# Bucketed attention and a feed-forward block: scores kept negated, a least in place of maximum and guard

## The chip, the cores and the metric

One of the eight cores of a Trainium2 chip runs the whole program. The metric is the device time of one execution in microseconds; a kernel's figure is the median of its timed runs. TensorE multiplies matrices from SBUF into PSUM, VectorE and ScalarE work on either memory, GpSimd only on SBUF, and SyncE issues most of the transfers. Each engine has its own queue of instructions and works it off in order; the engines wait for one another through semaphores.

## The reference

```python
batch, n_heads, seq, head_dim = (4, 8, 768, 64)         # q, k, v: float32; proj: 64 x 6
q_bits = (np.einsum('bhsd,dk->bhsk', q, proj) > 0).astype(np.int64)
k_bits = (np.einsum('bhsd,dk->bhsk', k, proj) > 0).astype(np.int64)
q_bucket = np.sum(q_bits * powers, axis=-1)             # six sign bits make a bucket
k_bucket = np.sum(k_bits * powers, axis=-1)
mask = q_bucket[:, :, :, None] == k_bucket[:, :, None, :]
scores = scale * np.matmul(q, k.transpose(0, 1, 3, 2))  # scale = 1/8
scores = np.where(mask, scores, -1000000000.0)
scores = scores - np.max(scores, axis=-1, keepdims=True)
attn = np.exp(scores)
attn = attn / (np.sum(attn, axis=-1, keepdims=True) + 1e-09)
attn_out = np.matmul(attn, v)
x = attn_out.transpose(0, 2, 1, 3).reshape(3072, 512)
h = x @ w_in                                            # 512 x 2048
g = 0.5 * h * (1.0 + erf(h / sqrt(2)))
out = g @ w_out                                         # 2048 x 512
```

A row of queries whose bucket holds no key has every score at -1e9; after the subtraction all are 0, and the row attends to all keys alike.

## The kernel before

**Tiles and stages.** The four batches follow one another, each with eight heads. For each head the function `head_early` (first batch) or `head` (the others) loads the transposed queries and keys, splits them into a rounded part and a remainder (tiles Aq, Ak, Bq, Bk), projects them on the hash vectors, takes the signs, and writes 12 further rows behind the 64 of Aq and Ak. These rows add 0 to a score where the buckets agree and a multiple of `-BIG` (2^34) where they do not. The constants are `fold`, which scales the query half by 1/8, and `off`, `flips` and the hash tiles.

A *unit* is one head's block of 128 queries, 192 in all. `unit` (line 872) lays down these steps: `scores`, four matmuls into a PSUM buffer `s` of two banks, of which there are two (line 887); `top`, the negated row maximum over 768 keys on VectorE (line 890), written to a spare column of the same buffer; `guard`, a second VectorE operation (line 894), which compares that maximum with `limit` (BIG/2) and leaves two columns in `rows`: factor 1 and the negated maximum, or 0 and 0 for a row without a key; `exps`, the exponential on ScalarE with this factor and bias as operands in memory and an accumulated row sum (line 900). The buffer `s` is free again after the exponential. In the first batch (`WHOLE`) the exponentials stay float32 and are transposed by TensorE (line 951); half a row block at a time, they are copied out of PSUM by ScalarE or VectorE (`affine`, lines 429 and 432). In the other batches they are divided by their sum, split into two float16 parts (lines 429, 432, 915) and transposed by DMA (line 922). `values` multiplies them with v (lines 1031, 1040).

The feed-forward block works on 256 tokens and half of the 2048 hidden units at a time: 24 groups of 96 matmuls with `w_in` (line 1243), Gelu on ScalarE, a split into float16 parts (lines 429, 432 and 1300), 48 matmuls with `w_out` (line 1322). The weights are decoded, scaled and split on VectorE during the first batches (lines 524 to 593).

**What sets the order.** The order is computed before the program is built. Every step is added to a `Plan` with an engine (or a choice of engines with a cost on each), a cost in microseconds, a key, the steps it needs and the buffer it takes. `Plan.order` then runs a list scheduler: whenever an engine is free it takes, of the steps that are ready, the one with the lowest key. The keys are made from the unit's number and the entries of the dictionary `PAR` (line 34): `QK`, `MX` and `EX` stand for scores, maximum, and guard with exponential. The order that comes out is each engine's instruction stream; at run time semaphores hold it to the data. So a changed cost or key can move steps on any engine, and can move a step with a choice, such as a copy, from one engine to another.

Of the kernel before, what the change touches and what calls it, by code (L numbers as in the profile page):

```python
# [10 lines left out]
F32 = mybir.dt.float32  # L11
# [217 lines left out]
def tile_bucket_attention_moe(  # L229
# [10 lines left out]
    nc = tc.nc  # L240
# [26 lines left out]
    NT = 8  # L267
# [32 lines left out]
    rows = const.tile([P, NT, 5], F32, tag="rows", name="rows")  # L300
# [30 lines left out]
    def buf(step):  # L331
        if bufs[step.takes][step.slot] is None:
            bufs["x"][step.slot] = ring(const, "x", [P, 2, NPAIR, TC], F16, 1, step.slot)[0]
        return bufs[step.takes][step.slot]
# [16 lines left out]
    limit = const.tile([P, 2], F32, tag="limit", name="limit")  # L351
    nc.gpsimd.memset(limit, BIG / 2)
    SPARE = 1000
    for t in bufs["s"]:
        nc.vector.memset(t[:, SPARE : SPARE + 1], 1.0)

    fold = const.tile([P, 1], F32, tag="fold", name="fold")
    nc.gpsimd.memset(fold[:D], SCALE)
    nc.gpsimd.memset(fold[D:], 1.0)

# [18 lines left out]
    for n, rr in enumerate((slice(0, D), slice(D, P))):  # L379
        twice = praw[rr, :NBIT].unsqueeze(1).to_broadcast([D, 2, NBIT])  # L380
        low, high = (
            hashes[rr, r0 + n * KR : r0 + n * KR + 2 * NBIT].rearrange("p (t b) -> p t b", t=2) for r0 in (0, D)
        )
        nc.gpsimd.tensor_copy(out=high, in_=twice)
        nc.gpsimd.tensor_tensor(out=low, in0=twice, in1=high.bitcast(F32), op=ALU.subtract)
# [7 lines left out]
        out=flips[KR:, 1:2], in0=flips[KR:, 0:1], scalar1=-BIG / 2, scalar2=-BIG / 2, op0=ALU.mult, op1=ALU.add  # L393
    )
    nc.gpsimd.tensor_scalar(
        out=flips[KR:, 0:1], in0=flips[KR:, 0:1], scalar1=BIG, scalar2=0.0, op0=ALU.mult, op1=ALU.add
# [302 lines left out]
    def head_early(b, h, i, key, clear, cl):  # L699
# [52 lines left out]
        lq = add_low(bq[D:], top, SCALE)  # L752
# [5 lines left out]
        for c0, c1 in ((0, TC), (TC, S)):  # L758
# [9 lines left out]
            def sign(n=n, box=box):  # L768
                nc.scalar.activation(
                    out=buf(space)[:HR, n], in_=buf(box[0])[:HR, : n.stop - n.start], func=AF.Sign, bias=off[:HR],  # L770
                )
# [8 lines left out]
        def mask_k():  # L780
            rows = buf(space)[KR : KR + 2 * NBIT]
            affine(r2.engine, ak[D : D + 2 * NBIT], rows, BIG / 2, -BIG / 2)
# [89 lines left out]
    def unit(t, i, qs, cl, whole, made, place):  # L872
# [3 lines left out]
        sc, nb, ssum, si, r = (st[:, k : k + 1] for k in range(5))  # L876

        def both(step):

            return buf(step).rearrange("p (b k) -> p b k", b=2)[:, :, : S // 2]  # L880
# [8 lines left out]
        def top():  # L889
            nc.vector.tensor_reduce(out=buf(sp)[:, SPARE + 1 : SPARE + 2], in_=both(sp), axis=AX.XY, op=ALU.max, negate=True)  # L890

        def guard():

            nc.vector.scalar_tensor_tensor(  # L894
                out=st[:, :2], in0=limit, scalar=buf(sp)[:, SPARE + 1 : SPARE + 2],
                in1=buf(sp)[:, SPARE : SPARE + 2], op0=ALU.is_gt, op1=ALU.mult,
            )

        def exps():
            nc.scalar.activation(  # L900
                out=buf(ex).rearrange("p (b k) -> p b k", b=2), in_=both(sp), func=AF.Exp, scale=sc, bias=nb,
                accum_out=sums[:, t : t + 1] if whole else ssum,
            )
# [24 lines left out]
        mx = add("DVE", 0.87, top, t - PAR[f"MX{cl}"], [sp])  # L928
        sh = add("DVE", 0.13, guard, t - PAR[f"EX{cl}"], [mx])
        ex = add("ACT", 0.98, exps, t - PAR[f"EX{cl}"], [sh], takes="p", table="exp")  # L930
# [483 lines left out]
```

## Time and profile before

| | |
|---|---|
| timed runs (3) | 875.90, 877.86, 878.99 us; median 877.86 |
| profiled execution | 875.6 us from first to last instruction (span) |
| TensorE matmuls | busy 837.4 us, 96% |
| VectorE | busy 692.7 us, 79%, 1345 instructions |
| ScalarE | busy 623.9 us, 71%, 1033 instructions |
| GpSimd | busy 186.9 us, 21% |
| transfers | 117.96 MB, 135 GB/s on average |

The profile's own time is its span; what lies before the first and after the last instruction is in the timed runs and not in it. PE is TensorE, DVE VectorE, ACT ScalarE, POOL GpSimd, SP SyncE; L890 is line 890. "Busy" is the time in which at least one instruction of the engine runs. Instructions of one engine overlap at their ends, so what one costs its engine is read from its start to the next one's start, which is less than its length.

### The profile page before, as it was taken

To read this page: it belongs to the slowest core of one execution; us is meant where nothing else is said; L and a number is where in the kernel's file an instruction comes from. 1 tells how busy PE (TensorE), PEld (TensorE's weight loads), DVE (VectorE), ACT (ScalarE), POOL (GpSimd) and SP (SyncE) were. 2 spreads that over 40 slices of the span, in tenths; PEclk is the share of its full clock that TensorE was granted. 3 is DMA by queue.
4 is the path that set the end of the run, shared out by engine and by line. 5 is a ranking of instruction groups with operands and counts; after the bars stand their busy time and mean duration, and the time that the engine had idled before them with its cause. 6 is when DMAs were issued, how large, how long until landed. Compare 5 with 4: busy or idle time off the path is not lost.

```text
span 875.6 us, 16917 instructions
## 1 busy us (share of the span) xinstructions
PE 837.4 (96%) x6428; PEld 610.5 (70%) x6428; DVE 692.7 (79%) x1345; ACT 623.9 (71%) x1033; POOL 186.9 (21%) x214
## 2 busy tenths in 40 slices
PE   3887998999999999999999999999999999999997
PEld 2766666776777776876777867777687687666663
DVE  8999999999998999898998998788888874112122
ACT  5878788788788888798878887768868764322321
POOL 6144332245323223031121112202112000000000
PEclk9999999999999999999999999999999999999999
DMA  8564654464889997777988896767677593000000
GB/s 270 190 168 145 191 147 127 109 144 77 178 176 165 211 210 146 156 137 133 190 169 173 168 184 128 141 150 146 112 162 133 110 168 73 25 1 25 1 25 24
DMA packets 270641, 117.96 MB, mean 135 GB/s; under 512 B 228768, under 2 KB 253344, under 8 KB 270560
## 3 DMA queue, kind: packets, MB, share of 16 engines
q1 hardware_dynamic: 270384, 116.88, 61.4%
q8 instruction: 50, 0.82, 0.4%
q14 instruction: 31, 0.25, 0.1%
q10 hardware_dynamic: 176, 0.00, 0.0%
HBM read 41.95 MB, written 6.29 MB: 55 GB/s over the span
## 4 chain that ended last, share of the span: by engine, by line
PE 76%; DVE 15%; ACT 3%; DMA 2%; issue 2%; POOL 1%; SPq 0%; ACTq 0%; DVEq 0%; POOLq 0%
PE hp L1322 27%; PE hp L1243 27%; PE s L887 12%; PE hp L1040 7%; DVE s L890 4%; ACT p L900 1%; PE hp L839 1%; PE hp L840 1%; DVE Win L593 1%; DVE Wout L529 1%; DVE rows L894 1%; DMA wbits<-w_in 1%; DMA pt<-hl 1%; DVE g L1300 1%; PE hp L1031 1%
## 5 line engine op out<-in xcount | busy, mean ns | idle before, releaser
L1243 PE MATMUL hp<-x,Win 128*128 128x256 f16 x2304 | 268.2, 273 | 0.0
L1322 PE MATMUL hp<-Wout,g 128*128 128x512 f16 x1152 | 265.8, 380 | 0.5 <-DVE g L1300 0.5
L1243 PEld LDWEIGHTS <-Win 128*128 128x128 f16 x2304 | 219.4, 98 | 42.0 <-issue 12.9
L1322 PEld LDWEIGHTS <-g 128*128 128x128 f16 x1152 | 106.1, 98 | 127.0 <-issue 13.4
L890 DVE TENSOR_REDUCE s<-s 128x1 f32<-128x768 f32 x192 | 180.9, 957 | 10.2 <-PE s L887 8.4
L900 ACT ACTIVATE p<-s,rows 128x768 f32<-128x768 f32 x147 | 145.1, 987 | 27.7 <-DVE rows L894 21.6
L887 PE MATMUL s<-Ak,Aq 128*128 128x384 f32 x360 | 138.8, 385 | 12.0 <-ACT p L900 10.6
L1300 DVE SCALAR_TENSOR_TENSOR g<-h,ffs,g 128x512 f16<-128x512 f32 x96 | 74.0, 781 | 83.5 <-ACT g L429 79.9
L887 PE MATMUL s<-Bk,Bq 128*128 128x384 f32 x360 | 122.2, 339 | 0.0
L1253 ACT ACTIVATE h<-hp,ffs 128x512 f32<-128x512 f32 x96 | 65.5, 683 | 79.2 <-PE hp L1243 78.8
L887 PEld LDWEIGHTS s<-Ak,Aq 128*128 128x128 f32 x360 | 68.4, 190 | 29.2 <-ACT p L900 19.0
L1040 PE MATMUL hp<-pt,vhl 128*64 128x256 f16 x1296 | 76.5, 274 | 1.8 <-DVE vhl L688 1.8
L1040 PEld LDWEIGHTS <-vhl 128*64 128x64 f16 x1296 | 68.5, 110 | 11.3 <-issue 8.9
L887 PEld LDWEIGHTS s<-Bk,Bq 128*128 128x128 f32 x360 | 68.7, 191 | 1.0
L915 DVE SCALAR_TENSOR_TENSOR wbits<-p,rows,wbits 128x768 f16<-128x768 f32 x54 | 55.4, 1027 | 1.5 <-ACT wbits L429 1.3
L915 DVE SCALAR_TENSOR_TENSOR hl<-p,rows,hl 128x768 f16<-128x768 f32 x45 | 45.7, 1018 | 5.7 <-ACT hl L429 4.8
L900 ACT ACTIVATE wbits<-s,rows 128x768 f32<-128x768 f32 x45 | 44.4, 986 | 7.2 <-PE hp L1243 3.8
L1278 ACT ACTIVATE h<-h 128x2048 f32<-128x2048 f32 (+1 forms) x25 | 46.1, 1843 | 0.4
L951 PE MATMUL hp<-ident,p 128*128 128x128 f32 x288 | 41.5, 276 | 2.7 <-DVE rb L432 1.4
L432 POOL TENSOR_SCALAR g<-h,ffs 128x512 f16<-128x512 f32 x28 | 25.0, 894 | 79.9 <-DVE rows L894 31.3
L429 ACT ACTIVATE pt<-hp 128x384 f32<-128x384 f32 x80 | 35.9, 486 | 6.5 <-PE hp L951 6.0
L432 POOL TENSOR_SCALAR Ak<-sign,flips 12x768 fp32r<-12x768 f32 x16 | 20.2, 1264 | 92.9 <-DVE sign L846 84.1
(199 smaller groups left out, 1113.5 us busy)
## 6 DMA issues: line engine op xcount, KB each, us to landing
raw<-qk SPq DMA_DIRECT2D x28, 384.0 KB, 3.8
vraw<-v SPq DMA_DIRECT2D x28, 384.0 KB, 4.2
wbits<-w_in SPq DMA_DIRECT2D x16, 512.0 KB, 4.2
wbits<-w_out SPq DMA_DIRECT2D x16, 512.0 KB, 3.6
out<-o SPq DMA_DIRECT2D x11, 512.0 KB, 2.9
Bk<-Bq SPq DMA_DIRECT2D x18, 192.0 KB, 2.7
Bq<-Aq SPq DMA_DIRECT2D x15, 192.0 KB, 3.4
Ak<-Aq SPq DMA_DIRECT2D x13, 192.0 KB, 2.9
```

Of the source, the lines that this page charges most:

```text
L432: on.tensor_scalar(out=out, in0=in_, scalar1=scale, scalar2=bias, op0=ALU.mult, op1=ALU.add)
L887: nc.tensor.matmul(to, x, y, start=k == 0, stop=k == 1)
L890: nc.vector.tensor_reduce(out=buf(sp)[:, SPARE + 1 : SPARE + 2], in_=both(sp), axis=AX.XY, op=ALU.max, negate=True)
L900: nc.scalar.activation(out=buf(ex).rearrange("p (b k) -> p b k", b=2), in_=both(sp), func=AF.Exp, scale=sc, bias=nb, accum_out=sums[:, t : ...
L915: nc.vector.scalar_tensor_tensor(out=buf(hi)[:, 1], in0=buf(ex), scalar=r, in1=buf(hi)[:, 0], op0=ALU.mult, op1=ALU.subtract,)
L951: nc.tensor.transpose(buf(step[0])[:, (k - k0) * P : (k - k0 + 1) * P], buf(ex)[:, words(k)], ident32,)
L1040: nc.tensor.matmul(pv[j * D : (j + 1) * D], buf(vh)[:, tv, kt, j * D : (j + 1) * D], buf(holds[j][0])[:, tp * KT + kt, :nt], start=kt == 0 ...
L1243: nc.tensor.matmul(buf(pair[0])[:, j * ch[1] : (j + 1) * ch[1]], win_hl[:, f0 // WB1, tw, pr, f0 % WB1 : f0 % WB1 + P], x[:, tx, pr, : ch[1]],
L1253: nc.scalar.activation(out=bufs["h"][0][:, 2 * fp : 2 * fp + 2, :nt], in_=buf(pair[0])[:, : 2 * nt].rearrange("p (j k) -> p j k", j=2), fu ...
L1278: nc.scalar.activation(out=h, in_=h, func=AF.Gelu)
L1300: nc.vector.scalar_tensor_tensor(out=gt[:, 1, s2, :nt], in0=h[:, s2, :nt], scalar=sg, in1=gt[:, 0, s2, :nt], op0=ALU.mult, op1=ALU.subtract,)
L1322: nc.tensor.matmul(buf(banks[u]), gt[:, tg, f, u * P : (u + 1) * P], wout_hl[:, ft // UT, tw, ft % UT], start=fresh and f == ti == 0, stop ...
```

## The change

The query half is scaled by -1/8 instead of 1/8, and the bucket rows change sign with it, so that PSUM holds the negated scores: small numbers where the buckets agree, and at least BIG more where they do not. One VectorE operation takes the smaller of each score and BIG/2, writes it back in place, and accumulates the least of the row into `nb`. The exponential then takes -1 as a constant factor and `nb` as its bias. A row without a key has BIG/2 everywhere, so every exponent is 0, as before. `top`, `guard`, `limit` and the spare column go. The signs of the early heads take a factor from memory (`turned`). The planner's costs for the two steps, and nearly all of its keys, are new.

```diff
-PAR = dict(DR_ACT=-182.94, DR_DVE=59.53, SI0=-589.8, SI1=-431.4, ...
+PAR = dict(DR_ACT=-116.64, DR_DVE=-333.22, SI0=-589.8, SI1=33.87, ...
...
-    rows = const.tile([P, NT, 5], F32, tag="rows", name="rows")
+    rows = const.tile([P, NT, 4], F32, tag="rows", name="rows")
...
-    limit = const.tile([P, 2], F32, tag="limit", name="limit")
-    nc.gpsimd.memset(limit, BIG / 2)
-    SPARE = 1000
-    for t in bufs["s"]:
-        nc.vector.memset(t[:, SPARE : SPARE + 1], 1.0)
...
-    nc.gpsimd.memset(fold[:D], SCALE)
+    nc.gpsimd.memset(fold[:D], -SCALE)
     nc.gpsimd.memset(fold[D:], 1.0)
+    turned = const.tile([2 * KR, 1], F32, tag="turned", name="turned")
+    nc.gpsimd.memset(turned[:KR], -1.0)
+    nc.gpsimd.memset(turned[KR:], 1.0)
...
-    for n, rr in enumerate((slice(0, D), slice(D, P))):
-        twice = praw[rr, :NBIT].unsqueeze(1).to_broadcast([D, 2, NBIT])
+    for n, (rr, n0) in enumerate(((slice(0, D), NBIT), (slice(D, P), 0))):
+        twice = praw[rr, n0 : n0 + NBIT].unsqueeze(1).to_broadcast([D, 2, NBIT])
...
-        out=flips[KR:, 1:2], in0=flips[KR:, 0:1], scalar1=-BIG / 2, scalar2=-BIG / 2, op0=ALU.mult, op1=ALU.add
+        out=flips[KR:, 1:2], in0=flips[KR:, 0:1], scalar1=BIG / 2, scalar2=BIG / 2, op0=ALU.mult, op1=ALU.add
...
-        out=flips[KR:, 0:1], in0=flips[KR:, 0:1], scalar1=BIG, scalar2=0.0, op0=ALU.mult, op1=ALU.add
+        out=flips[KR:, 0:1], in0=flips[KR:, 0:1], scalar1=-BIG, scalar2=0.0, op0=ALU.mult, op1=ALU.add
...
-        lq = add_low(bq[D:], top, SCALE)
+        lq = add_low(bq[D:], top, -SCALE)
...
-                    out=buf(space)[:HR, n], in_=buf(box[0])[:HR, : n.stop - n.start], func=AF.Sign, bias=off[:HR],
+                    out=buf(space)[:HR, n], in_=buf(box[0])[:HR, : n.stop - n.start], func=AF.Sign, scale=turned[:HR],
+                    bias=off[:HR],
...
-            affine(r2.engine, ak[D : D + 2 * NBIT], rows, BIG / 2, -BIG / 2)
+            affine(r2.engine, ak[D : D + 2 * NBIT], rows, -BIG / 2, BIG / 2)
...
-        sc, nb, ssum, si, r = (st[:, k : k + 1] for k in range(5))
+        nb, ssum, si, r = (st[:, k : k + 1] for k in range(4))
...
-        def top():
-            nc.vector.tensor_reduce(out=buf(sp)[:, SPARE + 1 : SPARE + 2], in_=both(sp), axis=AX.XY, op=ALU.max, negate=True)
-
-        def guard():
-
-            nc.vector.scalar_tensor_tensor(
-                out=st[:, :2], in0=limit, scalar=buf(sp)[:, SPARE + 1 : SPARE + 2],
-                in1=buf(sp)[:, SPARE : SPARE + 2], op0=ALU.is_gt, op1=ALU.mult,
+        def least():
+            nc.vector.tensor_scalar(
+                out=both(sp), in0=both(sp), scalar1=BIG / 2, scalar2=None, op0=ALU.min, op1=ALU.min, accum_out=nb,
             )
...
-                out=buf(ex).rearrange("p (b k) -> p b k", b=2), in_=both(sp), func=AF.Exp, scale=sc, bias=nb,
+                out=buf(ex).rearrange("p (b k) -> p b k", b=2), in_=both(sp), func=AF.Exp, scale=-1.0, bias=nb,
...
-        mx = add("DVE", 0.87, top, t - PAR[f"MX{cl}"], [sp])
-        sh = add("DVE", 0.13, guard, t - PAR[f"EX{cl}"], [mx])
-        ex = add("ACT", 0.98, exps, t - PAR[f"EX{cl}"], [sh], takes="p", table="exp")
+        mx = add("DVE", 0.96, least, t - PAR[f"MX{cl}"], [sp])
+        ex = add("ACT", 0.89, exps, t - PAR[f"EX{cl}"], [mx], takes="p", table="exp")
```

## Rows read from the trace of the kernel before

**Rows 1.** Busy us of each engine (instructions started) in stretches from:to us.
```profile
19.00:150.00 131.00, 115.29 (x852) 88.75 (x852) 128.46 (x265) 107.07 (x223) 45.27 (x44) 1.00 0.56 166
150.00:250.00 100.00, 96.24 (x748) 70.15 (x743) 95.17 (x197) 80.03 (x132) 36.72 (x37) 1.00 0.57 128
250.00:727.00 477.00, 476.23 (x3816) 353.46 (x3814) 422.85 (x810) 382.95 (x614) 93.13 (x110) 1.00 0.80 156
...
sum 876.00, PE 837.35 PEld 610.52 DVE 692.66 ACT 623.93 POOL 186.93; mean PE 139.56 PEld 101.75 DVE 115.44 ACT 103.99 POOL 31.16
```

**Rows 2.** The chain that ended last: shares of the span by engine.
```profile
PE 76%; DVE 15%; ACT 3%; DMA 2%; issue 2%; POOL 1%; SPq 0%; ACTq 0%; DVEq 0%; POOLq 0%
```

**Rows 3.** TensorE's waits from 0 to 250 us: us, times, longest.
```profile
PE s L887 <- ACT p L900: 12.2, 21, 1.3
```

**Rows 4.** Groups by line: shapes xcount | busy us, mean ns | idle before, releasers.
```profile
L890 DVE TENSOR_REDUCE s<-s 128x1 f32<-128x768 f32 x192 | 180.9, 957 | 10.2 <-PE s L887 8.4 <-PE hp L951 0.5 <-ACT diag L429 0.2
L900 ACT ACTIVATE p<-s,rows 128x768 f32<-128x768 f32 x147 | 145.1, 987 | 27.7 <-DVE rows L894 21.6 <-DVE hl L915 2.9 <-DVE tiny L409 0.8
...
L429 ACT ACTIVATE pt<-hp 128x384 f32<-128x384 f32 x80 | 35.9, 486 | 6.5 <-PE hp L951 6.0
```

**Rows 5.** The chain, 75 to 150 us: start us, us, what.
```profile
100.26 0.88 DVE s L890
...
101.17 0.23 DVE rows L894
...
113.36 0.13 DVE rows L894
```

**Rows 6.** VectorE in order of time: start us, length us, instruction.
```profile
27.07 0.97 DVE L890 TENSOR_REDUCE s<-s 128x1 f32<-128x768 f32 x1
...
28.54 0.22 DVE L894 SCALAR_TENSOR_TENSOR rows<-limit,s 128x2 f32<-128x2 f32 x1
...
39.00 0.17 DVE L991 RECIPROCAL shares<-sums 128x4 f32<-128x4 f32 x1
39.09 0.53 DVE L432 TENSOR_SCALAR pt<-hp 128x384 f32<-128x384 f32 x1
39.53 0.95 DVE L890 TENSOR_REDUCE s<-s 128x1 f32<-128x768 f32 x1
```

**Rows 7.** Groups by line and shape, as in rows 4.
```profile
L429 ACT ACTIVATE Aq<-raw,fold 128x768 fp32r<-128x768 f32 x20 | 18.6, 929 | 6.3 <-PE s L887 6.2
...
L429 ACT ACTIVATE Aq<-sign,flips 12x768 fp32r<-12x768 f32 x10 | 10.2, 1024 | 6.6 <-DVE sign L846 4.2 <-issue 1.4 <-DVE rows L909 1.0
...
L432 DVE TENSOR_SCALAR pt<-hp 128x384 f32<-128x384 f32 x16 | 8.6, 547 | 0.0
...
L432 DVE TENSOR_SCALAR rb<-hp 128x256 f32<-128x256 f32 x5 | 2.1, 412 | 0.0
```

**Rows 8.** ScalarE in order of time.
```profile
22.97 0.99 ACT L900 ACTIVATE p<-s,rows 128x768 f32<-128x768 f32 x1
23.86 0.19 ACT L900 ACTIVATION_READ_ACCUMULATOR p<-s,rows 128x1 f32 x1
23.95 0.48 ACT L429 ACTIVATE pt<-hp 128x384 f32<-128x384 f32 x1
```

**Rows 9.** The row maximum (L890) by stretch: VectorE busy us (count).
```profile
19.00:150.00 131.00, 43.28 (x46) 1.00 0.56 166
150.00:250.00 100.00, 22.55 (x24) 1.00 0.57 128
```

**Rows 10.** All engines in order of time, the first 30 us.
```profile
0.82 0.09 DVE L355 MEMSET s<- 128x1 f32 x2 [0.82 <-PEq L1403]
...
10.79 0.47 ACT L769 ACTIVATE sign<-hp,off 44x256 f32<-44x256 f32 x1 [1.36 <-PE hp L766]
```

**Rows 11.** The chain, 360 to 372 us.
```profile
361.95 1.32 PE hp L1243 x12
...
367.32 1.42 PE hp L1243 x12
```

More of the change, by code (lines that the diff above doesn't have):

```diff
@@ new lines @@
+PAR = dict(DR_ACT=-116.64, DR_DVE=-333.22, SI0=-589.8, SI1=33.87, SI2=600, SI_ACT=86.64, SI_DVE=-463.22, SI_Pool=-280.46, Z=257.45, VS0=-6.52, H0=575.6, HL=-75.74, VS=-5.3, G2=536.23, HQ=287.35, VQ=133.02, in0=-136.05, out0=39.44, in1=470.48, out1=-78.2, in2=233.28, out2=598.02, in3=240.84, out3=-463.72, H1=289.33, H2=438.91, H3=-445.9, H4=538.02, H5=-507.07, H6=-322.13, H7=-426.4, MEV=57.33, MGE=-266.31, MSP=582.63, V0=133.02, QK0=308.47, QK1=-234.44, QK2=-269.23, MX0=-109.89, MX1=-259.28, MX2=-600, EX0=477.71, EX1=387.36, EX2=-566.67, NR0=-144.91, NR1=-116.36, NR2=394.56, HI0=-417.18, HI1=144.81, HI2=-439.36, LO0=-350.93, LO1=214.11, LO2=418.95, PV0=-597.04, PV1=-520.42, PV2=-322.13, TR0=501.03, TR1=90.19, TR2=-590.8, V1=-436.5, V2=169.07, Sin0=379.14, Sin1=351.82, Sin2=508.84, Sin3=-255.14, Sout0=-176.43, Sout1=102.14, Sout2=-346.16, Sout3=188.34, Lin=269.75, Pin=377.13, Qin=-421.89, Cin=-600, Min=455.05, Lout=307.37, Pout=-115.77, Qout=-274.79, Cout=-216.53, Mout=339.83, G0=145.57, G1=316.52, G3=502.99, G4=274.38, G5=-52.33, G6=280.57, G7=-451.2, DUP0=-94.58, DUP1=-328.89, DUP2=-320.31, LOW0=-497.03, LOW1=-119.09, LOW2=500.78, PRJ0=-143.17, PRJ1=-512.55, PRJ2=-290.23, MSK0=522.69, MSK1=-11.73, MSK2=77.86, DI_ACT=-486.69, DI_DVE=100.43, DI_Pool=-394.49, WS_ACT=261.56, WS_DVE=-67.96, WS_Pool=-0.85, WH_ACT=18.86, WH_DVE=-320.98, WH_Pool=-560.31, WL_ACT=564.2, WL_DVE=-600, WL_Pool=-208.15, VH_ACT=-113.72, VH_DVE=394.66, VH_Pool=-584.38, MV_SP=-121.74, MV_ACT=138.2, MV_DVE=265.92, MV_Pool=440.5, LO_ACT=144.07, LO_DVE=311.43, LO_Pool=445.51, RND_ACT=469.84, RND_DVE=-296.69, RND_Pool=-340.91, MSK_ACT=595.62, MSK_DVE=66.63, MSK_Pool=-23.57, HI_ACT=-179.38, HI_DVE=455.51, HI_Pool=-12.15, EV_ACT=-66.36, EV_DVE=194.44, EV_Pool=-334.15, GH_ACT=120.65, GH_DVE=-153.54, GH_Pool=321.73, RB=-469.96, RS_ACT=93.05, RS_DVE=-364.96, RS_Pool=112.23, XH_ACT=-27.74, XH_DVE=-275.65, XH_Pool=11.3, XL_DVE=-458.38, XL_Pool=226.74, DUP3=-517.96, DUP4=236.89, DUP5=584.2, EX3=324.96, EX4=-372.4, EX5=-600, HI3=130.65, HI4=104.05, HI5=-279.61, LO3=430.46, LO4=479.15, LO5=45.97, LOW3=32.17, LOW4=-172.58, LOW5=-356.95, MSK3=-5.99, MSK4=311.24, MSK5=292.63, MX3=480.63, MX4=257.45, MX5=-581.8, NR3=-216.85, NR4=-574.93, NR5=345.12, PRJ3=377.13, PRJ4=180.25, PRJ5=210.32, PV3=-67.18, PV4=-452.92, PV5=211.67, QK3=89.17, QK4=399.99, QK5=99.55, SI3=266.44, SI4=573, SI5=515.21, TR3=-166.81, TR4=600, TR5=83.9, V3=111.74, V4=-181.97, V5=-188.93, Linb=328.05, Loutb=350.05, Pinb=109.11, Poutb=599.85, Qinb=259.04, Qoutb=355.37, Cinb=-101.97, Coutb=-451.52, Minb=100.86, Moutb=125.82, MVf_SP=6.12, MVf_ACT=343.18, MVf_DVE=-470.49, MVf_Pool=-600, LOf_ACT=319.76, LOf_DVE=600, LOf_Pool=-510.45, RNDf_ACT=-5.99, RNDf_DVE=-52.64, RNDf_Pool=-96.29, MSKf_ACT=-465.23, MSKf_DVE=304.16, MSKf_Pool=378.56)
```

1 line of the change is left out of this document (removed).

## The prediction

> **What bounds the kernel now.** I read busy time by stretch first [rows 1]. TensorE is busy 837.4 of the 875.6 us of the span, so all that a change off TensorE can win is 38.2 us. 15.7 of these lie between 19 and 150 us, 3.8 between 150 and 250 and 0.8 in the 477 us after that; the other 18 lie before 19 us, while the first heads are loaded and split, and at the very end. From 250 us on TensorE practically never lacks work, and a faster VectorE or ScalarE buys nothing there. From 19 to 150 us it is VectorE that is full, 128.5 of 131 us, with ScalarE at 107.1. The chain agrees: 15% of it, some 130 us, is VectorE [rows 2]. TensorE's own waits up to 250 us name the exponential that frees a scores buffer, 12.2 us in 21 waits [rows 3]; but the exponential waits for the guard, 21.6 us [rows 4], and the guard stands in VectorE's queue. So in the first stage a unit of attention is worth what it costs VectorE from the start of an operation to the start of the next.
>
> That price is read from the chain's pieces, which touch each other [rows 5]: the row maximum takes 0.88 us and, with another operation in between, its guard 0.13; 1.00 us together. Directly behind the maximum the guard starts 0.03 late and costs 0.23, since it must wait for the result. Mostly another operation stands in between, which costs the unit latency: the maximum of 27.07 us ends at 28.04, and its guard starts at 28.54 [rows 6].
>
> **The change, part by part.**
>
> *The one pass, `least`.* It goes over the same 768 elements of PSUM with one input and a constant, and writes them back. The nearest rows are VectorE's one-input copies out of PSUM: 547 ns for 384 elements and 412 for 256 [rows 7], 1.05 ns per element, so 768 last 547 + 384 x 1.05 = 950 ns, as long as the maximum's 957 [rows 4]. From start to start the 384-element copy takes 0.44 us [rows 6], so 768 take 0.44 + 0.40 = 0.84, and the maximum takes 0.88; I take 0.86. The accumulated least must also come out. The trace has no VectorE accumulator; ScalarE's exponential has one, with a row of its own, 0.19 us long, after which the next operation starts 0.09 later [rows 8]. A one-column operation of VectorE also takes 0.09 from start to start [rows 6]. So 0.86 + 0.09 = 0.95 us against 1.00: 0.05 saved per unit. The bounds: 0.14 saved if the least comes out for nothing; at the other end a write into the bank that is being read could cost a second pass, 0.80 more, so 0.75 lost. No row shows VectorE writing more than one column of PSUM. I keep 0.05, nearest to the rows of both parts. A page of the Trainium skill, "VectorE: DVE Perf Modes", in its section "Two Vector instructions with no wait between them", counts an operation that writes out its accumulator as two instructions, the pass and a read. By that rule VectorE keeps two instructions per unit, and the saving is the 0.05 already taken; without it the saving would be 0.14, and 6.4 us would stand for the first stage. No run here shows it for VectorE yet.
>
> 46 units have their maximum between 19 and 150 us, 24 up to 250 [rows 9], some 122 of the 192 after. First stage: 46 x 0.05 = 2.3 us. Where the guard stands directly behind its maximum (4 of the 46, counted along VectorE's rows; one is in [rows 5]) the wait of 0.13 goes too: 0.5 us. From 150 to 250 us VectorE is 95% busy and TensorE waits only 3.8 us; of 24 x 0.05 = 1.2 I count half, 0.6. The later units save 6 us of VectorE beside a full TensorE: nothing.
>
> *What comes earlier.* With one instruction the exponential no longer waits for a guard that is queued behind other work (0.5 us in the example of [rows 6], and 0.2 for the guard). That is latency: the scores buffer goes sooner, but VectorE has only 131 - 128.5 = 2.5 us of idle time in which to use it. Ends: 0 and 2.5; I take the middle, 1.2.
>
> *The exponential with a constant factor.* ScalarE's rows put a price on an operand held in memory: over 768 elements 929 ns with one, 1024 with two [rows 7]. The exponential has two (factor and bias) and lasts 987 [rows 4]; with one it lasts some 0.09 less, 17 us of ScalarE over 192 units. The early heads give some back: their 16 signs get a factor from memory, 16 x 0.09 = 1.4 us. In the first stage that leaves 46 x 0.09 - 1.4 = 2.7 us, on an engine with 24 us idle there. It is worth something only where the order moves VectorE's work to it: a copy of half a transposed row block takes 486 - 90 = 396 ns on ScalarE from start to start and 0.44 on VectorE, and 16 of the 96 such copies are VectorE's [rows 4, 6, 7]. Ends: 0, and 2.7 / 0.396 x 0.44 = 3.0 us. I take 1.0, nearer to zero, since 24 us of idle ScalarE have not drawn these 16 over so far.
>
> *The start.* Two signs, the first at 10.79 us, lie ahead of the first exponential [rows 10]; 2 x 0.09 = 0.2 us lost. Two memsets of one PSUM column, at 0.82 us, leave VectorE: it waits for loads then, so nothing. GpSimd loses one such memset and gains two, on an engine that is busy 187 us of the span [rows 1]. Turning the signs of `fold`, `flips`, the hashes and the masks changes constants of instructions that stay.
>
> *The new order.* All keys of the planner change. It keeps every matmul, so TensorE's 837 us stay but for the cost of changing operands: twelve matmuls of line 1243 take 1.42 us behind those of line 1040 and 1.32 behind scores [rows 11]. The attention products come in 36 runs, so parting or joining a few of them moves 2 us at most, either way. I enter 0.
>
> Sum: 2.3 + 0.5 + 0.6 + 1.2 + 1.0 - 0.2 = 5.4 us. The profiled execution spans 875.6 us; less 5.4 is 870.2. The timed runs have a median of 877.86, 2.3 above that span (launch, end and their own spread of 875.9 to 878.99); added back, 872.5 us.
>
> **Rivals.**
> 1. *Latency, not VectorE's throughput, holds the first stage.* Then the shorter way from scores to a free buffer takes away the 12.2 us that TensorE waits for exponentials: 877.9 - 12.2 = 865.7. For it: the waits name the exponential, and the guard reaches it late. Against: VectorE at 98%.
> 2. *No gain.* The accumulator's read costs what the guard did, and the order finds no use for ScalarE's time: 877.9 less some 0.5, within the noise. For it: the pass covers the same elements, and something small still follows it. Then the change does not do what it says, one pass for two.
> 3. *Slower: the accumulator's read waits out the pass,* as a guard directly behind a maximum does, 0.88 + 0.03 + 0.23 = 1.14 us [rows 5], and no other work can be put in between because the planner sees one operation. Place: the 46 units and half of the 24 before 250 us, 58 in all. Price: 58 x (1.14 - 0.95) = 11 us, so 872.5 + 11 = 883.5. It makes the kernel slower beyond the noise from 0.95 + 8/58 = 1.09 us per unit. Against it: ScalarE's accumulator read starts 0.10 before its pass has ended [rows 8].
> 4. *Slower by far: the write takes a second pass.* 46 x 0.75 = 35 us in the first stage, 24 x 0.75 less 5 of idle VectorE is 13, and 122 x 0.75 = 92 against 54 us of idle VectorE is 38: about 960.
>
> **How the numbers follow.** Forecast 0.46, with its own range 867 to 875.5; rival 1 0.16; rival 2 0.20; rival 3 0.14; rival 4 0.04. About 0.3%, or 2.6 us, is what a measurement of this kernel can tell from no change. Faster than that: the forecast but 0.03, rival 1, and 0.03 of rival 2: 0.62. Within it: the rest of these, 0.20. Slower: rivals 3 and 4, 0.18. For 8 in 10 I reach from 863, below rival 1, to 883, just short of rival 3; outside lie rival 4, half of rival 3, and an order that wins or loses more than is counted.
>
> **What would show it.** VectorE: 192 passes of some 950 ns at `least`, each with a short accumulator row that adds 0.09 us from start to start, and no guard; a pass of 1.7 us is rival 4, and 1.14 us or more from its start to the next operation's is rival 3. ScalarE: exponentials of some 895 ns. By stretch: TensorE's idle time between 19 and 250 us down from 19.5 to about 14, the waits for exponentials below 12.2 us, and TensorE busy for 837 us in all, within 2. I am wrong if TensorE's busy sum moves by more than that (then the order made the difference), or if VectorE is no longer full in the first stage and TensorE still waits as long.

## The result and the profile after

The changed kernel takes 867.32 us (median of 4 runs, 866.55 to 868.34) against 878.42 for the kernel before (4 runs): a ratio of 0.9876, with a 95% interval of 0.9858 to 0.9895. It is 11.1 us faster, inside the range of 863 to 883. The direction and the place were right, the size was not: the forecast was 5.4 us.

The changed kernel has other line numbers: `least` is 889, the exponential 894, scores 886, `affine` 427 and 430. First the stretches; the columns are those of [rows 1], with 0 to 19 us added. The line of the kernel before for that stretch:

```profile
0.00:19.00 19.00, 5.81 (x18) 3.46 (x19) 15.00 (x26) 8.62 (x12) 11.82 (x26) 1.00 0.86 283
```

The kernel after:

```profile
0.00:19.00 19.00, 3.44 (x9) 1.44 (x9) 11.83 (x19) 7.40 (x10) 13.73 (x27) 1.00 0.68 207
19.00:150.00 131.00, 121.78 (x876) 93.17 (x877) 123.30 (x264) 105.98 (x224) 46.23 (x49) 0.99 0.57 166
150.00:250.00 100.00, 99.26 (x803) 75.56 (x802) 97.78 (x208) 81.18 (x134) 39.31 (x38) 1.00 0.64 142
250.00:727.00 477.00, 475.71 (x3852) 354.33 (x3850) 388.93 (x764) 361.32 (x614) 152.04 (x154) 1.00 0.79 157
...
sum 876.00, PE 835.96 PEld 611.83 DVE 649.85 ACT 594.33 POOL 251.31; mean PE 139.33 PEld 101.97 DVE 108.31 ACT 99.05 POOL 41.88
```

TensorE's idle time (length of the stretch less its busy time), before and after: 15.7 and 9.2 us from 19 to 150; 3.8 and 0.7 from 150 to 250; 0.8 and 1.3 from 250 to 727; but 13.2 and 15.6 before 19 us. So 9.5 us are won where the forecast looked, and 2.4 are lost at the start. (The two profiled executions span 875.6 and 866.6 us, 9.0 apart and not 11.1: the changed kernel's is the slowest of its four.) TensorE's busy sum is 1.4 us lower, so the new order itself added or took next to no TensorE work. VectorE is no longer full in the first stage: 123.3 of 131 us, where it was 128.5. Its sum falls by 42.8 us, more than the pass can save; 33.9 of that lie from 250 to 727 us, where the new keys give GpSimd 59 us more.

The shares of the chain say the same ([rows 2] had VectorE at 15%):

```profile
PE 83%; DVE 6%; ACT 4%; DMA 2%; issue 1%; POOL 0%; DVEq 0%; ACTq 0%; POOLq 0%
```

TensorE's waits for exponentials up to 250 us, 12.2 us in 21 waits in [rows 3]:

```profile
PE s L886 <- ACT p L894: 4.2, 11, 0.8
```

The groups of instructions, to be laid beside [rows 4] and [rows 7]:

```profile
L889 DVE TENSOR_SCALAR_CACHE_REDUCE s<-s 128x768 f32<-128x768 f32 x192 | 182.8, 961 | 20.0 <-PE s L886 19.1 <-ACT pt L427 0.2
L894 ACT ACTIVATE p<-s,rows 128x768 f32<-128x768 f32 x147 | 132.0, 900 | 21.1 <-DVE s L889 11.0 <-DVE hl L909 4.2 <-DVE rows L903 2.3
L889 DVE DVE_READ_ACCUMULATOR s<-s 128x1 f32 x192 | 26.6, 139 | 0.0
L427 ACT ACTIVATE pt<-hp 128x384 f32<-128x384 f32 x70 | 31.5, 493 | 4.8 <-PE hp L944 4.5
L430 DVE TENSOR_SCALAR pt<-hp 128x384 f32<-128x384 f32 x26 | 13.7, 549 | 0.5 <-PE hp L944 0.5
```

The in-place pass is as long as the maximum was (961 and 957 ns), the exponential lasts 87 ns less, and the least comes out by a second instruction of its own. What that instruction costs is seen in VectorE's rows in order of time:

```profile
22.16 0.14 DVE L889 DVE_READ_ACCUMULATOR s<-s 128x1 f32 x1
22.16 1.25 DVE L532 SCALAR_TENSOR_TENSOR Win<-wbits,Win 128x512 int32<-128x512 int32 x1
...
36.98 0.95 DVE L889 TENSOR_SCALAR_CACHE_REDUCE s<-s 128x768 f32<-128x768 f32 x1
37.85 0.14 DVE L889 DVE_READ_ACCUMULATOR s<-s 128x1 f32 x1
37.85 0.55 DVE L430 TENSOR_SCALAR pt<-hp 128x384 f32<-128x384 f32 x1
38.32 0.95 DVE L889 TENSOR_SCALAR_CACHE_REDUCE s<-s 128x768 f32<-128x768 f32 x1
```

The next operation mostly starts in the same instant as the accumulator's read (22.16 and 22.16, 37.85 and 37.85), here 0.87 us after the pass began. Over the first 250 us the median from a pass to the next operation is 0.88 us, so a unit costs VectorE 0.88 where maximum and guard cost 1.00: 0.12 saved, not the 0.05 of the forecast.

The start. GpSimd now makes the key remainders of the first heads one behind the other. Two rows of it in order of time, then TensorE's first scores and VectorE's first pass:

```profile
13.85 2.12 POOL L450 TENSOR_TENSOR Bk<-rawe,Aq 64x768 fp32r<-64x768 f32 x1
15.93 2.27 POOL L450 TENSOR_TENSOR Bk<-raw,Aq 64x768 fp32r<-64x768 f32 x1
...
19.62 0.66 PE L886 MATMUL s<-Ak,Aq 128*128 128x384 f32 x1 [0.93 <-ACT Aq L427]
...
21.27 0.97 DVE L889 TENSOR_SCALAR_CACHE_REDUCE s<-s 128x768 f32<-128x768 f32 x1 [4.76 <-PE s L886]
```

In the kernel before VectorE makes these remainders, at 7.17 and 8.05 us, and the first scores start at 17.49:

```profile
7.17 0.95 DVE L452 TENSOR_TENSOR Bk<-rawe,Aq 64x768 fp32r<-64x768 f32 x1
...
17.49 0.52 PE L887 MATMUL s<-Ak,Aq 128*128 128x384 f32 x1
```

### The profile page after: what moved, and what is told of

Read it like the earlier page. It is cut to its first block, busy times and chain, and to the rows that moved or that the text cites. A ratio compares the mean times of both kernels' runs of the same rounds, so it can differ in the third digit from the quotient of the medians.

```text
span 866.6 us, 16923 instructions
## 1 busy us (share of the span) xinstructions
PE 836.0 (96%) x6428; PEld 611.8 (71%) x6428; DVE 649.8 (75%) x1297; ACT 594.3 (69%) x1025; POOL 251.3 (29%) x265
## 4 chain that ended last, share of the span: by engine, by line
PE 83%; DVE 6%; ACT 4%; DMA 2%; issue 1%; POOL 0%; DVEq 0%; ACTq 0%; POOLq 0%
PE hp L1315 28%; PE hp L1236 26%; PE s L886 13%; PE hp L1033 8%; PE hp L1024 3%; DVE s L889 2%; PE hp L944 2%; ACT p L894 1%; DMA pt<-hl 1%; PE hp L839 1%; PE hp L838 1%; DMA pt<-wbits 1%; ACT pt L427 0%; PE hp L544 0%; DVE Win L591 0%
## 5 line engine op out<-in xcount | busy, mean ns | idle before, releaser
L1236 PE MATMUL hp<-x,Win 128*128 128x256 f16 x2304 | 267.6, 273 | 0.0
L1236 PEld LDWEIGHTS <-Win 128*128 128x128 f16 x2304 | 220.4, 98 | 41.1 <-issue 10.3
L889 DVE TENSOR_SCALAR_CACHE_REDUCE s<-s 128x768 f32<-128x768 f32 x192 | 182.8, 961 | 20.0 <-PE s L886 19.1
L894 ACT ACTIVATE p<-s,rows 128x768 f32<-128x768 f32 x147 | 132.0, 900 | 21.1 <-DVE s L889 11.0
L430 DVE TENSOR_SCALAR g<-h,ffs 128x512 f16<-128x512 f32 x41 | 22.4, 551 | 84.6 <-PE hp L1315 77.3
L886 PEld LDWEIGHTS s<-Ak,Aq 128*128 128x128 f32 x360 | 68.6, 190 | 21.7 <-ACT p L894 12.5
L909 DVE SCALAR_TENSOR_TENSOR wbits<-p,rows,wbits 128x768 f16<-128x768 f32 x52 | 53.4, 1030 | 4.0 <-POOL wbits L430 2.4
L894 ACT ACTIVATE wbits<-s,rows 128x768 f32<-128x768 f32 x45 | 40.4, 898 | 8.4 <-DVE s L889 3.9
L430 POOL TENSOR_SCALAR wbits<-p,rows 128x768 f16<-128x768 f32 x27 | 27.9, 1034 | 42.3 <-DVE rows L903 23.4
L944 PEld LDWEIGHTS hp<-ident,p 128*128 128x128 f32 x288 | 32.8, 140 | 7.8 <-ACT pt L427 1.5
```

The source lines that it names most:

```text
L430: on.tensor_scalar(out=out, in0=in_, scalar1=scale, scalar2=bias, op0=ALU.mult, op1=ALU.add)
L886: nc.tensor.matmul(to, x, y, start=k == 0, stop=k == 1)
L889: nc.vector.tensor_scalar(out=both(sp), in0=both(sp), scalar1=BIG / 2, scalar2=None, op0=ALU.min, op1=ALU.min, accum_out=nb,)
L894: nc.scalar.activation(out=buf(ex).rearrange("p (b k) -> p b k", b=2), in_=both(sp), func=AF.Exp, scale=-1.0, bias=nb, accum_out=sums[:, t ...
L909: nc.vector.scalar_tensor_tensor(out=buf(hi)[:, 1], in0=buf(ex), scalar=r, in1=buf(hi)[:, 0], op0=ALU.mult, op1=ALU.subtract,)
L944: nc.tensor.transpose(buf(step[0])[:, (k - k0) * P : (k - k0 + 1) * P], buf(ex)[:, words(k)], ident32,)
```

## Experiments

Theory T: VectorE's time per unit, from start to start, sets the first stage, and the change wins what it takes off that. Rival L: what counts is the shorter way from the scores to a free buffer, with one instruction in place of two. Rival O: the new order makes the gain. Kernels "in the old order" keep the old keys and the old planner costs, so that each engine's instructions stand as before; `least` stands where the maximum stood, and nothing stands in the guard's place. Each time is the median of a kernel's own runs, and each ratio is to the kernel before on the same chip (877.5 to 878.4 us).

**The new operations in the old order.** Against the changed kernel:

```diff
-PAR = dict(DR_ACT=-116.64, DR_DVE=-333.22, ...
+PAR = dict(DR_ACT=-182.94, DR_DVE=59.53, ...
...
-        mx = add("DVE", 0.96, least, t - PAR[f"MX{cl}"], [sp])
-        ex = add("ACT", 0.89, exps, t - PAR[f"EX{cl}"], [mx], takes="p", table="exp")
+        mx = add("DVE", 0.87, least, t - PAR[f"MX{cl}"], [sp])
+        sh = add("DVE", 0.13, lambda: None, t - PAR[f"EX{cl}"], [mx])
+        ex = add("ACT", 0.98, exps, t - PAR[f"EX{cl}"], [sh], takes="p", table="exp")
```

> The order of every engine as in the kernel before; the one pass stands where the maximum stood, nothing where the guard stood, the exponential has its constant factor. Before has 878.4 us, the changed kernel 867.3. Theory T (VectorE's time in the first stage counts: its trace after shows 0.876 us from start to start for the pass and 0.00 for the accumulator's read, so 1.00 - 0.876 = 0.12 us per unit): 46 units and half of 24 make 58 x 0.12 = 7 us, so about 871. Rival L (the way from scores to a free buffer counts): the guard's queueing of 0.6 us goes as well, so most of the 12.2 us of waits, about 867. Rival O (the new order made the gain): 878, within 2.6 us of before.

Measured: 870.41 us, ratio 0.9913 (0.9898 to 0.9929). 7.8 of the 10.9 us between 878.2 and 867.3 come without the new order. O falls as the main cause; about 3 us are left for it.

**The pass alone, and the constant factor alone, in the old order.** The first gives the exponential of the last kernel its factor from memory, the second gives the kernel before a constant one (for rows without a key the guard's factor is left out):

```diff
-func=AF.Exp, scale=-1.0, bias=nb,
+func=AF.Exp, scale=minus, bias=nb,
...
-func=AF.Exp, scale=sc, bias=nb,
+func=AF.Exp, scale=1.0, bias=nb,
```

> As the first, but the exponential takes its factor -1 from memory, so ScalarE saves nothing. T: as the first within 1.5 us, about 871.5, since ScalarE has 24 us idle in the first stage. L: the exponential is 0.09 us longer on the way to the free buffer, 46 x 0.09 = 4 us worse than the first, about 871 where the first has 867. O: 878.

> The kernel before with one change: the exponential takes a constant factor 1, so the factor that the guard makes for rows without a key is left out; maximum and guard stay. T: no change, 878 within 2. L: the way to the free buffer is 0.09 us shorter in each of 46 to 58 units, 4 to 5 us less, about 874. O: 878.

Measured: 871.75 us, ratio 0.9922 (0.991 to 0.9934), and 876.49 us, ratio 0.998 (0.9971 to 0.9989). The pass is worth 6.5 us, or 54 us for each us that a unit costs VectorE (6.5 / 0.12); the constant factor 1.3 on top of it and 1.7 without it.

**VectorE's time put back, the way to the exponential left short.** Two kernels in the old order, with something idle in the guard's place that the exponential needs nothing of:

```diff
+        def idle():
+            nc.vector.scalar_tensor_tensor(out=junk, in0=halves, scalar=halves[:, :1], in1=halves, ...)
...
-        sh = add("DVE", 0.13, lambda: None, ...
+        sh = add("DVE", 0.13, idle, ...
```

```diff
+        def idle():
+            for _ in range(2):
+                nc.vector.memset(junk, 0.0)      # 32 columns
```

> As the first, but where the guard stood VectorE does an operation of the guard's shape (128x2) on constants, whose result nobody reads and which the exponential does not wait for. VectorE's load per unit is 0.876 + 0.13 = 1.01 us as before, the early release of the exponential stays. T: the gain of the first is gone, 877 to 878. L: the gain of the first stays but for 1 to 2 us. O: 878 like the first.

> As the dummy guard, with a fairer dummy: where the guard stood VectorE sets 32 columns of an unused tile to zero, twice, which reads nothing from SBUF and should cost 0.12 to 0.14 us from start to start like the guard. (The first dummy read two operands from SBUF and took up to 1.8 us beside GpSimd's operations, and came to 883.) T: VectorE's load is as before, so 877 to 879. L (the earlier exponential counts): like the first run but for 1 us, about 871.

The first: 883.35 us, ratio 1.0052 (1.0039 to 1.0064), slower than the kernel with the real guard, and no fair test of a guard's load. GpSimd's and VectorE's rows of that kernel show why:

```profile
23.38 1.81 POOL L453 TENSOR_TENSOR Bk<-raw,Aq 64x768 fp32r<-64x768 f32 x1
...
23.57 1.64 DVE L897 SCALAR_TENSOR_TENSOR junk<-halves 128x2 f32<-128x2 f32 x1
```

An operation over two columns, 0.22 us long in [rows 6], lasts 1.64 us and ends with GpSimd's subtraction (25.21 and 25.19). The real guard had a PSUM operand where this one has two in SBUF. The Trainium skill, "SBUF — State Buffer", section "Who interferes with whom", says that a VectorE operation with two SBUF inputs contends with a GpSimd operation that reads SBUF, over a pair of shared ports that only one of them holds at a time; these rows agree with it. From start to start the dummies cost 0.246 us on average over the first 250 us (median 0.13). At 54 us per us that is 13.3 us, and 870.4 + 13.3 = 883.7: the first dummy, too, costs what T makes of its real load.

The second has no SBUF input: 880.73 us (12 runs), ratio 1.0028 (1.0016 to 1.004). VectorE's rows of it, and the group of its exponentials, which are released by the pass (`s`):

```profile
26.93 0.24 DVE L896 MEMSET junk<- 128x32 f32 x2
27.15 0.97 DVE L890 TENSOR_SCALAR_CACHE_REDUCE s<-s 128x768 f32<-128x768 f32 x1
```

```profile
L899 ACT ACTIVATE p<-s,rows 128x768 f32<-128x768 f32 x147 | 131.9, 898 | 16.6 <-DVE s L890 10.0 <-DVE hl L914 3.4 <-DVE wbits L914 1.2
```

The pair costs 0.18 us on average over the first 250 us and 0.01 more where it meets an accumulator's read (below), so 0.19. It takes back 880.7 - 870.4 = 10.3 us, 54 per us of load, the same price as before, although no exponential needs the memsets. The time lies above T's 877 to 879 because the pair costs 0.19 us and not the 0.13 of a guard. T stands and L falls: no gain from latency alone is seen.

**The new order with the old operations, and the new costs with the old keys.** The first puts a minimum by `tensor_reduce` and the guard, back to back, into the step of `least` and gives the exponential its factor from memory; the second only takes the old `PAR`:

```diff
-            nc.vector.tensor_scalar(out=both(sp), in0=both(sp), scalar1=BIG / 2, ..., accum_out=nb)
+            nc.vector.tensor_reduce(out=buf(sp)[:, SPARE + 1 : SPARE + 2], in_=both(sp), axis=AX.XY, op=ALU.min)
+            nc.vector.scalar_tensor_tensor(out=st[:, :2], in0=limit, ..., op0=ALU.is_gt, op1=ALU.mult)
...
-scale=-1.0, bias=nb,
+scale=sc, bias=nb,
```

> The changed kernel's order and negated scores, with the old operations in the place of the one pass: least of the row into a spare column and, directly behind it, the guard, whose factor (-1 or 0) and bias the exponential takes from memory. The two stand back to back, so a unit costs VectorE 0.88 + 0.03 + 0.23 = 1.14 us where it could cost 1.00. T (what a unit costs VectorE up to 250 us decides): 58 x (1.14 - 0.88) = 15 us above the 867.3 of the changed kernel, 882, so slower than before although the order is the new one. O (the order made the gain): below 872. With the first four runs: new operations alone gave 7.8 of the 11 us, so the order should be worth about 3 when the operations are the new ones.

> The changed kernel with all keys of the kernel before: new operations, new planner costs, and an order that follows from the old keys. If the gain were the operations' whatever the order, about 870, like the first run. If an order holds only for the costs that its keys were fitted to, as the list scheduler's changes of mind suggest, it is worse than the first run by far: 880 or more.

Measured: 893.23 us, ratio 1.0175 (1.0159 to 1.0191), and 896.04 us, ratio 1.0208 (1.0191 to 1.0225). The new order is no gain by itself: with the old operations it loses 15 us. Nor do the old keys suit the new costs: that kernel's TensorE waits 18.1 us for exponentials over the whole span, against 5.3 in the changed kernel, and 20 us of it (57.7 to 64.5, 115.7 to 119.1 and 221.5 to 231.7) run at half the granted clock. A set of keys belongs to the costs that it was made for. T's 882 for the first was 11 us short; the next kernels say why.

**The constant factor in the new order.** The changed kernel with `scale=minus` from memory, its order unchanged.

> The changed kernel, but the exponential takes its factor -1 from memory: each one 0.09 us longer, 17 us of ScalarE in all, nothing else. In the old order this cost 1.3 us (871.75 against 870.41). T: as little in the new order, 868 to 869.5. If the new order makes use of ScalarE's time, as the 17 us would suggest: 871 or more.

Measured: 872.71 us, ratio 0.9943 (0.993 to 0.9957). The same 90 ns on each exponential (990 and 900) cost 1.3 us in the old order and 5.4 in this one. Passes 1, 49, 65 and 129 of VectorE, first in the changed kernel:

```profile
21.27 0.97 DVE L889 TENSOR_SCALAR_CACHE_REDUCE s<-s 128x768 f32<-128x768 f32 x1 [4.76 <-PE s L886]
...
153.53 0.95 DVE L889 TENSOR_SCALAR_CACHE_REDUCE s<-s 128x768 f32<-128x768 f32 x1
...
234.99 0.96 DVE L889 TENSOR_SCALAR_CACHE_REDUCE s<-s 128x768 f32<-128x768 f32 x1
...
451.48 0.96 DVE L889 TENSOR_SCALAR_CACHE_REDUCE s<-s 128x768 f32<-128x768 f32 x1
```

and in the kernel with the factor in memory:

```profile
21.29 0.97 DVE L891 TENSOR_SCALAR_CACHE_REDUCE s<-s 128x768 f32<-128x768 f32 x1 [4.76 <-PE s L888]
...
155.38 0.95 DVE L891 TENSOR_SCALAR_CACHE_REDUCE s<-s 128x768 f32<-128x768 f32 x1
...
237.40 0.96 DVE L891 TENSOR_SCALAR_CACHE_REDUCE s<-s 128x768 f32<-128x768 f32 x1
...
455.49 0.95 DVE L891 TENSOR_SCALAR_CACHE_REDUCE s<-s 128x768 f32<-128x768 f32 x1
```

The second falls behind by 1.85 us over the first 48 units, 2.41 by the 65th and 4.01 by the 129th. The loss comes little by little and goes on to 450 us, long after the first stage: in the new order ScalarE's time is on the way there too, in the old order hardly.

**VectorE's time put back in the new order.** The two memsets ahead of the pass, or behind it, within the step of `least`:

```diff
         def least():
+            for _ in range(2):
+                nc.vector.memset(junk, 0.0)      # second kernel: behind the pass
             nc.vector.tensor_scalar(out=both(sp), in0=both(sp), ..., accum_out=nb)
```

> The changed kernel in its own order, with two memsets of 32 spare columns on VectorE ahead of every pass, inside the same step: they cost VectorE about 0.18 us per unit from start to start (measured in the old order), and the exponential still waits for the pass alone. Theory T (VectorE's time per unit sets the first stage; 54 us per us of load, as the old order showed): 867.3 + 0.18 x 54 = 877. Rival N (the new order is packed tighter, so that a us of load costs what the old maximum and guard cost in it, (893.2 - 867.3) / 0.257 = 101): 867.3 + 18 = 885.5. Rival L (only the way from the scores to the exponential counts): the memsets mostly run before the scores are there, so within 3 us of 867.3.

> The same two memsets behind the pass instead of ahead of it, same step, same load. If the exponential is released by the pass, T and N expect the time of the kernel with the memsets ahead, within 2 us. If the time of the old maximum and guard in the new order came from the later release of the exponential (0.26 us), and the trace shows the exponential waiting for the memsets, this kernel is clearly slower than the one with the memsets ahead.

Measured: 882.06 us, ratio 1.0041 (1.0027 to 1.0055), and 885.08 us, ratio 1.0079 (1.0058 to 1.01); between T's 877 and N's 885.5. VectorE's rows of the second in order of time, and the group of its exponentials:

```profile
37.83 0.14 DVE L890 DVE_READ_ACCUMULATOR s<-s 128x1 f32 x1
37.91 0.24 DVE L894 MEMSET junk<- 128x32 f32 x2
38.07 0.52 DVE L431 TENSOR_SCALAR pt<-hp 128x384 f32<-128x384 f32 x1
```

```profile
L897 ACT ACTIVATE p<-s,rows 128x768 f32<-128x768 f32 x147 | 131.9, 898 | 29.9 <-DVE junk L894 18.6 <-DVE hl L912 5.6 <-DVE wbits L912 1.5
```

A memset behind an accumulator's read starts 0.08 us after it (37.83 and 37.91), where other operations start with it. So the pair ahead adds 0.20 us per unit on average (0.18, and 0.09 in the 10 units of 66 where it follows another pass), and the pair behind 0.255 (0.08 and 0.17). The prices are (882.06 - 867.32) / 0.20 = 74 and (885.08 - 867.32) / 0.255 = 70 us per us. In the second the exponential does wait for the memsets, 18.6 us in all, and yet a us costs no more than in the first: L falls in this order as well. Against the kernel with the factor in memory, the old operations (0.99 + 0.14 = 1.13 us, 0.257 more than the pass) cost (893.23 - 872.71) / 0.257 = 80. So T's 882, which is about the load at the old order's price (867.3 + 0.257 x 54 = 881), missed two things: the factor in memory, 5.4 us, and a price of 70 to 80 in the new order. The two kernels with memsets are 3.0 us apart, more than the 2 that the expectation allowed if the pass released the exponential; but the pair behind is also 0.055 us more load, at 70 some 3.9 us.

Where the added time comes in is seen from the passes of the 65th and the last unit. First the old order: the kernel before, and the one with the pass alone.

```profile
232.38 0.96 DVE L890 TENSOR_REDUCE s<-s 128x1 f32<-128x768 f32 x1
...
723.13 0.96 DVE L890 TENSOR_REDUCE s<-s 128x1 f32<-128x768 f32 x1
```

```profile
226.94 0.97 DVE L891 TENSOR_SCALAR_CACHE_REDUCE s<-s 128x768 f32<-128x768 f32 x1 [0.17 <-PE s L888]
...
717.64 0.96 DVE L891 TENSOR_SCALAR_CACHE_REDUCE s<-s 128x768 f32<-128x768 f32 x1
```

Then the new order: the last pass of the changed kernel (its 65th, at 234.99, stands above), and both passes with the memsets ahead and with the memsets behind.

```profile
663.09 0.96 DVE L889 TENSOR_SCALAR_CACHE_REDUCE s<-s 128x768 f32<-128x768 f32 x1 [0.30 <-PE s L886]
```

```profile
246.34 0.94 DVE L892 TENSOR_SCALAR_CACHE_REDUCE s<-s 128x768 f32<-128x768 f32 x1
...
677.84 0.94 DVE L892 TENSOR_SCALAR_CACHE_REDUCE s<-s 128x768 f32<-128x768 f32 x1
```

```profile
246.57 0.95 DVE L890 TENSOR_SCALAR_CACHE_REDUCE s<-s 128x768 f32<-128x768 f32 x1
...
680.05 0.96 DVE L890 TENSOR_SCALAR_CACHE_REDUCE s<-s 128x768 f32<-128x768 f32 x1
```

In the old order the pass alone is 5.4 us ahead at the 65th unit and 5.5 at the last: nothing comes in between. (The memsets of the old order, against the new operations in it, are 7.0 us behind at the 65th unit and 8.7 at the last, so a little can come late there too.) In the new order the memsets are 11.4 and 11.6 us behind at the 65th unit, and 14.8 and 17.0 at the last. So up to the 65th unit a us of VectorE's load costs much the same in both orders, 5.4 / 0.12 = 45 in the old and 11.4 / 0.20 = 57 and 11.6 / 0.255 = 45 in the new. Most of what makes the new order dearer comes in after it, 3.4 and 5.4 us; for the old operations against the factor in memory it is 11.4 us by the 65th unit and 21.7 by the last. N's tighter packing is not seen in the first stage.

**The start.** The changed kernel with the key remainders of the first two heads moved from GpSimd to VectorE:

```diff
     steps = plan.order()
+    for low, after in zip(first_low[::2], first_low[1::2]):
+        low.engine = "DVE"
+        steps.remove(low)
+        steps.insert(steps.index(after) + 1, low)
```

> The changed kernel with one move: the key remainders of the first two heads, which the new order gives to GpSimd (2.12 and 2.27 us, done at 15.97 and 18.2 us), are done by VectorE (0.95 us each) right behind its own remainders of these heads, at about 8 to 10 us. TensorE's projection, which waits 7.5 us for the first of them, can start some 6 us earlier; the first scores (19.6 us) then wait for the masks and the key copy of GpSimd, some 4 us earlier. T with a first stage bound by VectorE: its idle time before its first pass (4.8 us) goes for the most part, less 1.9 us that it takes on: 2 to 3 us faster than the changed kernel, 864 to 865. If the start is covered (what is gained there is lost again to the loads or to GpSimd): 867.

Measured: 864.22 us, ratio 0.9846 (0.9832 to 0.9859): 3.1 us faster than the changed kernel, as T expected, and the fastest of all. Its rows of VectorE and TensorE:

```profile
7.18 0.95 DVE L451 TENSOR_TENSOR Bk<-rawe,Aq 64x768 fp32r<-64x768 f32 x1
...
15.94 0.69 PE L891 MATMUL s<-Ak,Aq 128*128 128x384 f32 x1 [5.27 <-POOL Ak L431]
...
17.62 0.97 DVE L894 TENSOR_SCALAR_CACHE_REDUCE s<-s 128x768 f32<-128x768 f32 x1 [1.20 <-PE s L891]
```

The first pass starts at 17.62 us instead of 21.27, and these 3.65 us come through nearly whole. The new order's late start was a loss that the total hid.

## Why the prediction was right in kind and wrong in size

- **What bounds the kernel: right for the first 250 us.** In either order VectorE's load shows up in the time, and load taken away pays it back. 58 units (the 46 of the first stage and half of the next 24) was the forecast's own count; the old order's 54 us per us is near it, and so are the 45 to 57 that either order shows up to the 65th unit. That VectorE and ScalarE buy nothing from 250 us on holds nearly in the old order and fails in the new one, where 3.4 and 5.4 us of the memsets' cost come in later.
- **The one pass: the step that failed.** Its 0.95 us was 0.86 for the pass, which measured 0.88, and 0.09 for the accumulator's read, which measured 0.00 behind a pass with reading work after it. The read was sized from ScalarE's accumulator and from one-column operations [rows 6, 8]; neither row shows VectorE's. The bound for "comes out for nothing", 0.14, was the nearest. With 0.12 the forecast's own sum would have been 46 x 0.12 + 12 x 0.12 + 0.5 = 7.5 us against 6.5 measured, instead of 3.4. The rule cited there from the Trainium skill, "VectorE: DVE Perf Modes", section "Two Vector instructions with no wait between them", two instructions for an operation that writes out its accumulator, is borne out (192 passes, 192 reads of 139 ns); what I drew from it, that the second costs a slot, is not.
- **What comes earlier, 1.2 us: not found.** The exponential's release can be left short or made long; within an order the price per us of VectorE load stays about the same.
- **The exponential's constant factor, 1.0 us:** 1.3 in the old order, 5.4 in the new. The way in which I saw it come in was wrong too. Copies of half a transposed row block did not move to ScalarE but to VectorE (16 to 26).
- **The start, 0.2 us lost:** 2.4 more idle us before 19, and 3.1 won back by undoing it. I counted what the diff adds at the start and not what the new keys move there: GpSimd's remainders.
- **The new order, entered at 0:** about 3 us in all (870.41 and 867.32), but that is no property of the order by itself. With the factor in memory the two orders are 1.0 us apart, the new one slower (871.75 and 872.71); with the old operations it is 15 us slower. The 10.9 us are thus 6.5 for the pass, 1.0 lost to the order, and 5.4 for the constant factor in it. The order is fitted to the cheaper operations, makes VectorE's time dearer over the whole program (70 to 80 against 54), and turns ScalarE's saving into time. The bound of 2 us on changing operands held: the 36 attention products stand in 29 unbroken runs before and in 24 after, and TensorE's busy sum moved by 1.4. The result lies just inside the forecast's own range, 867 to 875.5, and so do the operations alone, 870.4. That the order, entered at nothing, takes only 3 us off is luck: without its late start it takes off 6 (864.22), outside that range.
- **Rivals.** The latency rival named 865.7, close to the result, for a reason that the memsets refute. Rivals 3 and 4 are refuted by the pass, 0.95 to 0.97 us long, and by the read that starts with the next operation; rival 2 by the 6.5 us of the pass alone. Of the forecast's own signs, TensorE's busy sum stayed within 2 us; its idle time between 19 and 250 us fell from 19.5 to 9.9, further than the 14 that was forecast.

Open: why this order lets VectorE's and ScalarE's time through after 250 us, while TensorE is busy for over 99% of the 477 us after it in both kernels. Part of the answer may be what "busy" says. In the changed kernel the group of line 1236, the matmuls with `w_in`, reads

```profile
L1236 PE MATMUL hp<-x,Win 128*128 128x256 f16 x2304 | 267.6, 273 | 0.0
```

Each lasts 273 ns, but they overlap and take 267.6 / 2304 = 0.116 us apiece, so a start that is late by up to 0.16 us shows as busy time (an estimate from this row). From the 129th to the last pass the kernel with the memsets behind runs as many matmuls as the changed kernel (1702) and takes 3.9 us longer, of which only 1.4 are idle time. Which wait makes them late was not traced.

The prices are rough, too. Several of these kernels run parts of their first 250 us at TensorE's lower clock (below): the changed kernel, the one with the factor in memory and the one with the memsets behind for 3.4 us each, the one with the memsets ahead and the old operations in the new order for three times 3.4. At half the clock 3.4 us can cost 1.7 at most, so up to 3.4 us of these last two kernels' times may be the clock's: the 74 is then 57 to 74, the 80 is 67 to 80, and the 70 is not touched by it.

## What to carry to other kernels

Price an operation by the gap from its start to the next one's, and when a new instruction form has no row in the trace, let the range carry both ends and ask which operation will follow it. Where a change comes with a new order, test the operations in the old order and the old operations in the new one: here each saving had two prices, and only the pair shows it. To see where a price is paid, compare the start of the same unit's operation in two traces. And look at the first 20 us by themselves, since a list scheduler with new keys can start late while the total still falls.

## What the hardware did that I had not expected

- VectorE's read of its accumulator is 139 ns long and cost 0.00 us in front of operations that read data, 0.08 us in front of a memset.
- Writing 768 columns back into the PSUM that is being read cost nothing: 961 ns against 957 for the maximum, which writes one column.
- TensorE's granted clock is 1.2 GHz, the lower of its two levels, for a few us early in some kernels. In the changed kernel the granted share is 0.51 from 30 to 33.4 us, where matmuls ran after 1.6 idle us in the 3 before (0.96 us at 27.04, 0.64 at 28.55):

```profile
30.00:33.40 3.40, 3.40 (x13) 2.42 (x12) 2.26 (x4) 2.61 (x5) 0.36 (x1) 0.51 0.43 117
```

  The kernel with the earlier start has no such stretch between 20 and 250 us; the old operations in the new order have three, in their profiled execution, and so has the kernel with the memsets ahead.
